# Gated attention mix on one core: the weights' last 64 rows written to both partition halves by one transfer, and one rounding step moved ahead of two evictions

## The chip, the cores and the metric

The kernel runs on one core of one Trainium2 chip. The metric is the device time of one execution in microseconds; the time before is the median of three runs.

## The reference

Two attention blocks read the same `x` (2048 positions, 448 features, 16 heads of 28), and a sigmoid gate mixes their results. Block A attends to 8 positions two apart, backwards; block B attends to all positions. Cut to what matters:

```python
g = sigmoid((x * gate_w).sum(-1, keepdims=True))
# A: q, k, v = x @ A_wqkv; position s sees s, s-2, ..., s-14 (those >= 0)
a = softmax8(q . k[s - 2w] * 28**-0.5) . v[s - 2w] @ A_wo
# B: q, k, v = x @ B_wqkv; all positions, 16 heads
b = softmax(q @ k.T * 28**-0.5) @ v @ B_wo
out = g * a + (1 - g) * b
```

## The kernel before

**Split numbers.** A float32 operand of TensorE is kept as two tiles: `hi`, rounded to the matmul's type by ScalarE, and `lo`, what is left of it, made by VectorE or GpSimd (`split`: one ScalarE activation, then one subtraction). A product takes three matmuls per block of 128 features: hi·hi, hi·lo and lo·hi.

**Features.** 448 features are three blocks of 128 rows (`kt` 0 to 2) and a tail of 64 rows (`kt` 3). The tail tile has 128 partitions: for `x` one half of the partitions holds the hi part of the 64 rows and the other half the lo part, and the weights' 64 tail rows stand in both halves. One matmul over 128 partitions then does hi·hi and lo·hi of the tail. So each weight tail is loaded twice, into partitions 0 to 63 and 64 to 127; `both` does that. `xh[nb]` and `xl[nb]` hold `x` in four blocks of 512 positions; they are loaded raw into slices of the tile `V` (`load_x`, `load_tails`) and split by `split_x(nb)`, whose kt 3 step is a 64-row activation on ScalarE and a 64-row subtraction on VectorE.

**The start.** SyncE (SP) issues, in this order: three blocks of the first weights, the tail of x block 0, the first weights' tail for columns 448 to 703 (`both`, into `wt0`), `wr1` (384 weight rows for columns 0 to 127), their tail (`both`), the tail of x block 1, then x block 1 (`load_x(1)`), block 2, the tails of blocks 2 and 3, block 3. ScalarE's own queue issues x block 0. All of SP's transfers share one queue, and each of the eight semaphores that the transfers signal is used in turn, so that SP waits, before a transfer, until the one eight places earlier has landed.

**The projections.** `tiles` lists the output tiles. Tiles 0 to 9 are projected whole (`project`); tiles 0 and 1 are interleaved product by product in the order `FIRST`, which takes kt 3 last. Tiles 0, 1 and 2 use x block 0, tiles 3 to 5 block 1, tiles 6 and later blocks 2 and 3. Tile n goes to PSUM bank `PS[n % 4]`, is evicted by `qk_tile` (one ScalarE activation, L361, one VectorE subtraction, L362) and stored to DRAM by two transfers. Both evictions of tiles 0 and 1 stand after tile 1's place in the loop, followed by `split_x(1)`, which takes kt 3 first, then 0, 1, 2. From tile 10 on the two row halves go to two banks at once (`project_halves`), and from tile 11 on S1 matmuls (L148) are put between them: a first pass of scores that finds each row's maximum, for which `KH` and `QP` are read back from DRAM. Later weights are loaded and split by `load_w` and `split_w` at tile numbers that `loads` and `splits` give; each tail goes through `both`.

**After the projections.** 256 steps each compute a piece of block B's scores (L991), their exponentials (ScalarE) and the product with V (L957), while GpSimd and VectorE work on block A from a list; the last part multiplies by the output weights. The order of the instructions on each engine is that of the code: nothing is rearranged when the kernel runs.

Of the kernel before, what the change touches and what calls it, by code (L numbers as in the profile page):

```python
# [25 lines left out]
def gated_mix_kernel(ctx: ExitStack, tc: tile.TileContext, xT, xn, gw, wA, wB, woAB, out):  # L26
    nc = tc.nc
# [170 lines left out]
    def max_turn(t):  # L198
        r = sp.tile([128, 32], F32, name="nms")
        nc.vector.transpose(r, t.bitcast(F32))  # L200
        return r
# [18 lines left out]
    with tc.tile_pool(name="xp", bufs=1) as xp, tc.tile_pool(name="wp", bufs=2) as wp:  # L220
# [3 lines left out]
        def raw3():  # L224
            return wp.tile([128, 3, 450], F32, tag="raw", name="raw", bufs=2)

        def split(hi, lo, raw, eng=nc.vector):
            nc.scalar.activation(hi, raw, AF.Copy)
            eng.tensor_tensor(out=lo, in0=raw, in1=hi.bitcast(F32), op=ALU.subtract)


        def both(dst, src, eng=nc.sync):
            for h in (0, 64):
                eng.dma_start(dst[h:h + 64], src)


        xst = V.rearrange("p j h e -> p (j h e)").rearrange("p (b k c) -> p b k c", b=NB, k=4)
# [10 lines left out]
        LOW = [slice(64, 128)] * 2 + [slice(0, 64)] * 2  # L248
        HIGH = LOW[2:] + LOW[:2]

        def split_x(nb):
            r, t = xst[:, nb, 0:3, :], xst[:, nb, 3, :]
            tail = xh[nb][:, 3, :]
            o, i = LOW[nb], HIGH[nb]
            for kt in (3, 0, 1, 2) if nb == 1 else range(4):
                if kt < 3:
                    split(xh[nb][:, kt, :], xl[nb][:, kt, :], r[:, kt, :])
                else:
                    nc.scalar.activation(tail[i], t[i], AF.Copy)
                    nc.vector.tensor_tensor(out=tail[o], in0=t[i], in1=tail[i].bitcast(F32), op=ALU.subtract)  # L260
# [3 lines left out]
        def load_w(wi, tails=(False, True)):  # L264
            src, cols = WSRC[wi]
            if wi not in wraw:
                wraw[wi] = raw3(), wp.tile([128, 450], F32, tag="wt", name="wt"), sum(c1 - c0 for c0, c1 in cols) + 2 * (wi == GATE)
            r, t, _ = wraw[wi]
            for tail in tails:
                o = 0  # L270
                for c0, c1 in cols:
                    e = o + c1 - c0
                    if tail:
                        both(t[:, o:e], src[384:448, c0:c1])
                    else:
                        nc.sync.dma_start(r[:, :, o:e], src[0:384, c0:c1].rearrange("(k p) c -> p k c", p=128))
                    o = e

                if wi == GATE:
                    if tail:  # L280
                        both(t[:, o:o + 2], gw[0:2, 384:448].rearrange("i p -> p i"))
                    else:
                        for kt in range(3):
                            nc.sync.dma_start(r[:, kt, o:o + 2],
                                              gw[0:2, 128 * kt:128 * kt + 128].rearrange("i p -> p i"))

        def split_w(wi, kts):
            if wi not in wsets:
                wsets[wi] = [wp.tile([128, 4, 450], F32R, tag=g, name=f"{g}{wi}") for g in ("wh", "wl")]
            wh, wl = wsets[wi]  # L290
            r, t, n = wraw[wi]
            for kt in kts:
                split(wh[:, kt, :n], wl[:, kt, :n], r[:, kt, :n] if kt < 3 else t[:, :n], nc.gpsimd)
# [24 lines left out]
        def project(n):  # L318
            if n == 0:
                for m, p in FIRST:  # L320
                    product(m, p, None, p == (0, 0, 0), p == (0, 1, 3))
            elif n > 1:
                for i, p in enumerate(ORDER):
                    product(n, p, None, i == 0, i == len(ORDER) - 1)
# [4 lines left out]
        def project_halves(n, s1):  # L329
            if n % 2 == 0:  # L330
                for m in (n, n + 1):
                    low = (tiles[m][2] if tiles[m][1] == "qk" else tiles[m][-1] // 4) < 2
                    for half in range(2):
                        l = [p for p in ORDER if p != (0, 1, 3) or half == (0 if low else 1)]
                        l = [(m, product, (m, p, half, i == 0, i == len(l) - 1)) for i, p in enumerate(l)]
                        if s1[m - n]:
                            l[8:8] = [(m, s1_half, (1, half))]
                            l[2:2] = [(m, s1_half, (0, half))]
                        todo[half] += l
            while any(l and l[0][0] == n for l in todo):  # L340
                for l in todo:
                    if l:
                        _, f, x = l.pop(0)
                        f(*x)
# [32 lines left out]
        def add_halves(n, dst, gate=None):  # L377
            raw = pair("raw")
            cols = D + 2 * (gate is not None)
            nc.scalar.activation(raw[:, :, 0:cols], PJ[n % 2][:, :, 0:cols], AF.Copy)  # L380
            nc.gpsimd.tensor_tensor(out=dst, in0=raw[:, 0, 0:D].rearrange("p (c e) -> p c e", e=dst.shape[-1]),  # L381
                                    in1=raw[:, 1, 0:D].rearrange("p (c e) -> p c e", e=dst.shape[-1]), op=ALU.add)
            if gate is not None:
                nc.gpsimd.tensor_tensor(out=gate, in0=raw[:, 0, D:D + 1], in1=raw[:, 1, D:D + 1], op=ALU.add)
# [38 lines left out]
        r, t = xst[:, 0, 0:3, :], xst[:, 0, 3, :]  # L423
# [35 lines left out]
        for n, t in enumerate(tiles):  # L459
            wi = t[0]  # L460
            for w in loads:
                if loads[w] == n:
                    load_w(w)
            for w in splits:
                i, k = (n - splits[w][0]) * splits[w][1], splits[w][1]
                if 0 <= i < 4:
                    split_w(w, range(i, i + k))
            if n in (3, 5):
                split_x((n + 1) // 2)
            if n < FULL:  # L470
                project(n)
            else:
                project_halves(n, [S1_START <= m < S1_START + 80 for m in (n, n + 1)])
            if t[1] == "qk":
                for m in {0: (), 1: (0, 1)}.get(n, (n,)):
                    qk_tile(m, *tiles[m][2:4])
            elif t[1] == "v":
                add_halves(n, V[:, t[2], :, 0:DH])
            else:
                a_tile(n, t[2], t[3])  # L480
            if n == 1:
                split_x(1)
            if n == 4:
                for t in QP[1]:
                    nc.scalar.activation(t, t0, AF.Copy)
            while fini and fini[0][0] <= n:
                fini.pop(0)[1]()
            if n in (2, 3):
                load_w(1, (n == 3,))
            if n == 3:  # L490
                load_qhi(0)
            if n in (3, 8):
                load_k(0, KH[0], qk_hi, slice(0, 1024) if n == 3 else slice(1024, S))
            if n == 16:
                for i in (1, 2):
                    nc.sync.dma_start(a_scr[i][:, 0:NJ, :].rearrange("c j e -> c (j e)").rearrange(
                        "c (a b) -> c a b", b=NJ), omg[0:8, None, :].to_broadcast([8, 56, NJ]))
            if n == 32:
                nc.gpsimd.memset(V[:, :, :, DH:], 1.0)
            if n == 22:  # L500
                load_k(1, KH[1], qk_hi)
            if n == 62:
                load_k(0, KL[0], qk_lo)
            if parts and parts[0][0] <= n:
                _, u, t = parts.pop(0)
                max_store(u, max_turn(t))
            if finished and n < len(tiles) - 3:
                u = finished.pop(0)
                parts.append((n + 3, u, max_parts(u)))
            if n == 64:  # L510
                gate = []
                for sgn, dst in ((-1.0, g_t), (1.0, omg)):
                    e = sp.tile([128, NJ], F32, name="ez")
                    nc.scalar.activation(e, zt, AF.Exp, scale=sgn)
                    nc.gpsimd.tensor_tensor(out=e, in0=e, in1=V[:, 0, :, DH], op=ALU.add)
                    gate.append((dst, e))
            if n in (66, 68):
                nc.vector.reciprocal(*gate.pop(0))
            if n == 70:
                nc.sync.dma_start(og_scr.rearrange("(j p) -> p j", j=NJ), omg)  # L520
            if n == 76:
                load_q(0)
# [70 lines left out]
    for nme in ("k", "v"):  # L593
        for i in range(2):
            t = a1.tile([128, HALO + NJ, 56], F32, name=f"{nme}t{i}")
# [110 lines left out]
    for c in range(8):  # L706
# [20 lines left out]
        n = 0  # L727
# [278 lines left out]
    for u in range(NU):  # L1006
        g, b = divmod(u, NB)
        for kt in range(NJ):
# [22 lines left out]
            if finished:  # L1031
                v = finished.pop(0)
                t = max_parts(v, (lambda f: at("end", st + 1, f)) if v < NU - 1 else None)
# [56 lines left out]
```

## Time and profile before

| | |
|---|---|
| median of three runs | 901.62 us (900.81 to 901.74) |
| the profiled execution | 900.95 us |
| its span in the profile | 899.2 us |
| TensorE matmul (PE) | busy 892.3 us, 99% |
| VectorE (DVE) | busy 739.0 us, 82% |
| ScalarE (ACT) | busy 643.1 us, 72% |
| GpSimd (POOL) | busy 639.7 us, 71% |
| granted TensorE clock | 1.0 |

The times in the rows are microseconds from the start of the span. In a row of the timeline stand the start, the time from the start to the end of the merged instructions, the engine, the line, the operation, out<-in, sizes and a count; a bracket at the end tells how long the engine was idle before it and what released it. PE is the matmul, PEld the loading of the stationary operand, SPq the issue of a transfer by SyncE. A DMA share is the mean busy share of the core's 16 DMA engines; it can exceed 1 because packets on an engine overlap.

### The profile page before, as it was taken

How to read it: one execution, taken by the hardware profiler on the slowest of the kernel's cores; microseconds unless marked ns; L12 is line 12 of the kernel's file. 1: busy time of each engine (PE TensorE's matmuls, PEld its weight loads, DVE VectorE, ACT ScalarE, POOL GpSimd, SP SyncE). 2: the span in 40 equal slices, each digit the busy share in tenths (PEclk: the TensorE clock that was granted, in tenths of full speed). 3: DMA queues.
4: the chain of work that ended last, by engine and by line, in shares of the span. 5: the costliest groups of instructions: out<-in, count | busy, mean ns of one | idle time of the engine just before them, and what ended most of it. 6: DMA issues, size and time to landing. Idle time of an engine off the chain costs nothing.

```text
span 899.2 us, 20532 instructions
## 1 busy us (share of the span) xinstructions
PE 892.3 (99%) x8323; PEld 525.1 (58%) x8323; DVE 739.0 (82%) x961; ACT 643.1 (72%) x765; POOL 639.7 (71%) x506
## 2 busy tenths in 40 slices
PE   9999999999999999999999999999999999999998
PEld 6888999998954444444444444444444444434997
DVE  6588999998979999999999999989999999832220
ACT  7456434343378898988988989889889898897220
POOL 1499847464459689999999999999999698501000
PEclk9999999999999999999999999999999999999999
DMA  8877403559472341226225242352220322337691
GB/s 268 284 256 197 138 12 84 143 136 95 123 239 73 100 127 46 70 57 156 70 56 145 84 115 64 88 136 65 53 64 18 94 43 56 96 81 208 183 272 52
DMA packets 115975, 104.51 MB, mean 116 GB/s; under 512 B 77177, under 2 KB 84217, under 8 KB 115097
## 3 DMA queue, kind: packets, MB, share of 16 engines
q1 hardware_dynamic: 115448, 102.42, 42.6%
q8 instruction: 65, 1.06, 0.5%
q10 hardware_dynamic: 432, 0.79, 0.3%
q14 instruction: 30, 0.24, 0.1%
HBM read 62.20 MB, written 40.96 MB: 115 GB/s over the span
## 4 chain that ended last, share of the span: by engine, by line
PE 94%; POOL 2%; DMA 1%; ACT 1%; DVE 0%; issue 0%; SPq 0%; POOLq 0%; ACTq 0%
PE T L991 29%; PE av L957 26%; PE r L316 15%; PE r L311 8%; PE T L837 8%; PE r L148 5%; PE T L148 4%; DMA rbc<-rs 1%; POOL prod L670 1%; POOL oat L675 1%; DMA vt<-a_scr 0%; POOL prod L614 0%; PE r L217 0%; ACT P L996 0%; ACT raw L380 0%
## 5 line engine op out<-in xcount | busy, mean ns | idle before, releaser
L996 ACT ACTIVATE P<-T 128x1024 f32<-128x1024 f32 x512 | 496.8, 1023 | 60.4 <-PE T L991 58.4
L154 DVE TENSOR_REDUCE MX<-T 128x1 f32<-128x512 f32 x470 | 441.8, 953 | 34.2 <-PE T L148 18.2
L957 PE MATMUL av<-P,V 128*32 128x512 f32 x2048 | 272.7, 605 | 0.0
L991 PEld LDWEIGHTS T<-QH,KH 30*128 30x128 f32 x1024 | 92.2, 181 | 231.1 <-ACT P L996 197.0
L148 PE MATMUL T<-KH,QP 28*128 28x512 f32 x704 | 219.9, 455 | 0.1
L991 PE MATMUL T<-QH,KH 30*128 30x512 f32 x1024 | 212.1, 489 | 0.6 <-DVE MX L154 0.4
L170 DVE TENSOR_REDUCE MX<-r 128x2 f32<-128x1024 f32 x160 | 192.5, 1221 | 23.9 <-PE r L148 19.9
L991 PE MATMUL T<-QH,KL 28*128 28x512 f32 x1024 | 186.7, 395 | 0.0
L991 PE MATMUL T<-QL,KH 28*128 28x512 f32 x1024 | 184.5, 392 | 0.0
L614 POOL TENSOR_TENSOR prod<-qt,kt 128x896 f32<-128x896 f32 x64 | 135.4, 2116 | 5.5 <-DMA kt<-a_scr 5.4
L380 ACT ACTIVATE raw<-r 128x896 f32<-128x896 f32 (+1 forms) x64 | 58.9, 921 | 98.0 <-PE r L316 96.4
L148 PE MATMUL r<-KH,QP 64*128 64x512 f32 x320 | 105.6, 391 | 0.0
L675 POOL TENSOR_TENSOR oat<-oat,prod 128x896 f32<-128x896 f32 x48 | 101.3, 2110 | 2.0
L148 PEld LDWEIGHTS T<-KH,QP 28*128 28x128 f32 x704 | 86.0, 181 | 27.2 <-ACT P L996 19.5
L381 POOL TENSOR_TENSOR ast<-raw 128x448 f32<-128x448 f32 x48 | 55.4, 1154 | 59.2 <-ACT raw L380 51.7
L670 POOL TENSOR_TENSOR prod<-vt,L 128x896 f32<-128x896 f32 x56 | 95.3, 1701 | 0.2
L316 PE MATMUL r<-wh,xh 64*128 64x448 f32 (+1 forms) x512 | 93.7, 363 | 0.9 <-ACT raw L380 0.9
L991 PEld LDWEIGHTS T<-QL,KH 28*128 28x128 f32 x1024 | 94.5, 184 | 0.0
L991 PEld LDWEIGHTS T<-QH,KL 28*128 28x128 f32 x1024 | 93.2, 183 | 0.3
L957 PEld LDWEIGHTS av<-P,V 128*32 128x32 f32 x2048 | 40.3, 107 | 77.7 <-issue 65.3
L316 PEld LDWEIGHTS r<-wh,xh 64*128 64x128 f32 x512 | 74.0, 185 | 4.0 <-ACT raw L380 1.3
L316 PE MATMUL r<-wh,xl 64*128 64x448 f32 (+1 forms) x384 | 73.6, 364 | 0.0
(114 smaller groups left out, 1115.6 us busy)
## 6 DMA issues: line engine op xcount, KB each, us to landing
a_scr<-ast SPq DMA_DIRECT2D x24, 448.0 KB
qk_hi<-qkh SPq DMA_DIRECT2D x24, 256.0 KB
qk_lo<-qkh SPq DMA_DIRECT2D x24, 256.0 KB
rbc<-rs SPq DMA_DIRECT2D x64, 64.0 KB
QP<-qk_hi SPq DMA_DIRECT2D x64, 56.0 KB
KL<-qk_lo SPq DMA_DIRECT2D x16, 224.0 KB
QH<-qk_hi SPq DMA_DIRECT2D x64, 56.0 KB
QL<-qk_lo SPq DMA_DIRECT2D x64, 56.0 KB
```

Source lines behind the costliest of these rows:

```text
L148: nc.tensor.matmul(bank, qhis[u][h % 2][r, 128 * qs:128 * qs + 128], KH[u // NB % 3][r, 512 * kc:512 * kc + 512], start=True, stop=True)
L154: i = nc.vector.tensor_reduce(MX[:, n % NMX:n % NMX + k], bank, axis=X, op=ALU.max)
L170: nc.vector.tensor_reduce(m, PM[k], axis=X, op=ALU.max)
L311: nc.tensor.matmul(bank, ws[c][rows, k, t[4]:t[4] + 128], x, start=first, stop=last)
L316: nc.tensor.matmul(bank[:, 0:cols], x, ws[c][rows, k, 0:cols], start=first, stop=last)
L614: nc.gpsimd.tensor_tensor(out=p, in0=qt[c], in1=kvt["k", c % 2][:, HALO - DIL * w:HALO - DIL * w + NJ, :], op=ALU.mult)
L670: nc.gpsimd.tensor_tensor(out=dst.rearrange("p j (h d) -> p j h d", d=DH), in0=kvt["v", c % 2][:, HALO - DIL * w:HALO - DIL * w + NJ, :].r ...
L675: nc.gpsimd.tensor_tensor(out=ows[c % 2][:, :, 0:56] if w == W - 1 else oat[c], in0=oat[c], in1=oat[c, w], op=ALU.add)
L837: writes(bank, nc.tensor.matmul(bank[:, :D], src, wo[c][k], start=(first and k == ks[0] and i == 0), stop=(last and k == ks[-1] and i == 2)))
L957: nc.tensor.matmul(av[32 * h:32 * h + 32, :], V[:, kt, 4 * g + h, :], tiles_[h], start=(kt == 0), stop=(kt == NJ - 1), skip_group_check=True)
L991: nc.tensor.matmul(bank[a], (KH[g % 3], KH[g % 3], KL[g % 2])[t][r, ks], (qh, ql, qh)[t][r, :], start=(t == 0), stop=(t == 2))
L996: e = nc.scalar.activation(p, one if a == "2" else mine, AF.Exp, scale=SCALE).ins
```

## The change

**One transfer in place of two.** `both(dst, src)` issued two transfers of 64 rows, one for each half of the partitions. Now it issues one with the whole tile of 128 partitions as its destination; its source is the same 64 rows taken twice, by a leading step of 0 with a count of 2. It is used nine times, so that nine transfers stand where 18 stood: two at the start, two for the two column pieces of weight set 1, one for each of sets 2 to 6. The gate's tail column is still loaded by two transfers.

**One step moved.** `split_x(1)`, called after tile 1's evictions, is cut in two: its kt 3 step now stands after the projection of tiles 0 and 1 and ahead of their evictions, its kt 0 to 2 steps where they were. Blocks 2 and 3 keep their order.

```diff
         def both(dst, src, eng=nc.sync):
-            for h in (0, 64):
-                eng.dma_start(dst[h:h + 64], src)
+            eng.dma_start(dst, src[None].to_broadcast([2, *src.shape]))
...
-        def split_x(nb):
+        def split_x(nb, kts=range(4)):
             r, t = xst[:, nb, 0:3, :], xst[:, nb, 3, :]
             tail = xh[nb][:, 3, :]
             o, i = LOW[nb], HIGH[nb]
-            for kt in (3, 0, 1, 2) if nb == 1 else range(4):
+            for kt in kts:
...
                     if tail:
-                        both(t[:, o:o + 2], gw[0:2, 384:448].rearrange("i p -> p i"))
+                        for h in (0, 64):
+                            nc.sync.dma_start(t[h:h + 64, o:o + 2], gw[0:2, 384:448].rearrange("i p -> p i"))
...
+            if n == 0:
+                split_x(1, (3,))
             if t[1] == "qk":
                 for m in {0: (), 1: (0, 1)}.get(n, (n,)):
                     qk_tile(m, *tiles[m][2:4])
...
             if n == 1:
-                split_x(1)
+                split_x(1, range(3))
```

SyncE's queue at the start, first as it stood before (`raw` and `wr` are weights, `wt` a weight tail, `V` holds raw x; the sizes are those of the destination):

```order
L409 DMA raw<-in_wB 128x256 x3
L244 DMA V<-in_xT 64x512
L234 DMA wt_191<-in_wB 64x256 x2
L413 DMA wr_192<-in_wB 128x3x128
L234 DMA wt_191<-in_wB 64x128 x2
L244 DMA V<-in_xT 64x512
L240 DMA V<-in_xT 128x3x512 x2
```

and as it stands now:

```order
L409 DMA raw<-in_wB 128x256 x3
L243 DMA V<-in_xT 64x512
L233 DMA wt_191<-in_wB 128x1x256
L413 DMA wr_192<-in_wB 128x3x128
L233 DMA wt_191<-in_wB 128x1x128
L243 DMA V<-in_xT 64x512
L239 DMA V<-in_xT 128x3x512 x2
```

The order is the same with two transfers fewer: `wr1`, the second tail and x block 1 each stand one or two places nearer to the front, and each `wt` transfer now covers 128 partitions.

ScalarE between the last split of the first weights and x block 1 (`wh` the weights' hi tile, `qkh` an evicted tile, `xh_181` x block 1, `xh_182` block 2), before:

```order
L228 ACTIVATE wh_188<-wt_191 128x256
L228 ACTIVATE wh_188<-wr_192 128x3x128
L228 ACTIVATE wh_188<-wt_191 128x128
L361 ACTIVATE qkh<-r_128 128x512
L361 ACTIVATE qkh<-r_132 128x512
L259 ACTIVATE xh_181<-V 64x512
L228 ACTIVATE xh_181<-V 128x512 x3
```

and now:

```order
L228 ACTIVATE wh_188<-wt_191 128x256
L228 ACTIVATE wh_188<-wr_192 128x3x128
L228 ACTIVATE wh_188<-wt_191 128x128
L258 ACTIVATE xh_181<-V 64x512
L361 ACTIVATE qkh<-r_128 128x512
L361 ACTIVATE qkh<-r_132 128x512
L228 ACTIVATE xh_181<-V 128x512 x3
```

The 64-row activation of x block 1 went two places up, ahead of the evictions of tiles 0 and 1; VectorE's 64-row subtraction moved in the same way ahead of its two L362 rows. TensorE's order is unchanged.

## The prediction

> **What bounds the kernel now.** I read the page first (busy shares, then the chain), and then the busy times by stretch.
>
> ```profile
> PE 892.3 (99%) x8323; PEld 525.1 (58%) x8323; DVE 739.0 (82%) x961; ACT 643.1 (72%) x765; POOL 639.7 (71%) x506
> ...
> PE 94%; POOL 2%; DMA 1%; ACT 1%; DVE 0%; issue 0%; SPq 0%; POOLq 0%; ACTq 0%
> ```
>
> ```profile
> 60.00:230.00 170.00, 169.08 (x1591) 157.44 (x1589) 153.43 (x137) 74.37 (x104) 110.90 (x118) 1.00 0.52 123
> ```
>
> TensorE is busy 99% of the span and carries 94% of the chain; from 60 to 230 us it works 169.08 of 170 us at a granted clock of 1.00. There is no idle time later in which a delay could be taken up, and none to be saved but at the start: whatever shifts TensorE's first tiles shifts the end by as much. So the change is worth what it does in the first 35 us. There I read the timeline of each engine.
>
> ```profile
> 8.76 0.40 ACT L228 ACTIVATE wh<-wt 128x256 fp32r<-128x256 f32 x1
> 9.07 0.51 ACT L228 ACTIVATE wh<-wr 128x384 fp32r<-128x384 f32 x1
> 9.48 0.30 ACT L228 ACTIVATE wh<-wt 128x128 fp32r<-128x128 f32 x1
> 10.92 1.09 ACT L361 ACTIVATE qkh<-r 128x512 fp32r<-128x512 f32 x2 [1.14 <-PE r L311]
> 11.89 0.62 ACT L259 ACTIVATE xh<-V 64x512 fp32r<-64x512 f32 x1
> 12.74 1.67 ACT L228 ACTIVATE xh<-V 128x512 fp32r<-128x512 f32 x3 [0.23 <-DMA V<-in_xT]
> ```
>
> ```profile
> 11.64 0.88 PEld L311 LDWEIGHTS r<-xh,wl 128*128 128x128 f32 x4
> 12.57 0.65 PEld L311 LDWEIGHTS r<-xl,wh 128*128 128x128 f32 x3
> 13.42 0.19 PEld L311 LDWEIGHTS r<-xh,wh 128*128 128x128 f32 x1 [0.20 <-ACT xh L228]
> 13.94 0.19 PEld L311 LDWEIGHTS r<-xh,wh 128*128 128x128 f32 x1 [0.33 <-ACT xh L228]
> 14.46 0.30 PEld L311 LDWEIGHTS r<-xh,wh 128*128 128x128 f32 x2 [0.34 <-ACT xh L228]
> ```
>
> Tile 3, the first that needs x block 1, starts at 13.42 and waits three times for ScalarE's rounding of that block: 0.20 + 0.33 + 0.34 = 0.87 us. ScalarE in turn waited 0.23 us for the block to land, at 12.74. Before that it sat idle 1.14 us ahead of the evictions, and then did the 64-row step (0.62) that the change moves.
>
> **The moved step.** It is 0.62 us on ScalarE, put into an idle 1.14.
>
> ```profile
> 10.64 0.29 DVE L229 TENSOR_TENSOR wl<-wt,wh 128x128 fp32r<-128x128 f32 x1
> 11.55 1.29 DVE L362 TENSOR_TENSOR qkh<-r,qkh 128x512 fp32r<-128x512 f32 x2 [0.62 <-ACT qkh L361]
> 12.87 0.68 DVE L260 TENSOR_TENSOR xh<-V,xh 64x512 fp32r<-64x512 f32 x1
> ```
>
> On VectorE it is 0.68 into an idle 0.62, so the evictions could be 0.06 late; their banks are next written by tile 4, three tiles on, so that costs nothing. The move frees ScalarE at 10.92 + 1.09 = 12.0 instead of 12.5; it pays only if block 1 has landed by then. What the move adds is a wait: behind the 64-row step on ScalarE now stand both evictions, block 1's rounding and all later tiles, and the step waits for the tail of block 1. So everything hangs on when transfers land.
>
> **The merged transfers.** Each saves SyncE an issue:
>
> ```profile
> 2.71 2.42 SPq L234 DMA_DIRECT2D wt<-in_wB  x2
> 5.18 0.59 SPq L413 DMA_DIRECT2D wr<-in_wB  x1
> 5.82 1.17 SPq L234 DMA_DIRECT2D wt<-in_wB  x2
> 7.03 0.59 SPq L244 DMA_DIRECT2D V<-in_xT  x1
> 7.92 0.91 SPq L240 DMA_DIRECT2D V<-in_xT  x2
> ```
>
> Two issues of 1.17 / 2 = 0.59 us go from in front of block 1 (issued at 7.92), some 1.2 us. But the bytes stay the same, and the question is how they are dealt over the 16 engines. Before, each tail was two transfers with 64 as the outermost count on both sides: 4 rows on each engine, twice. Now the destination's outermost count is 128, and the source's is 2, the two copies of the same 64 rows. If the source's count decides, two engines carry 64 rows each and 14 carry none. No row of this trace has a transfer with such unlike sides; the nearest are loads of `KH` and `KL` with an outermost count of 28, which 16 does not divide. Two stretches that hold little else give these shares of the 16 engines, the first from 287.8 to 291 us, the second from 317.6 to 321:
>
> ```profile
> q1 hardware_dynamic: 123, 0.67, 89.2%
> ...
> KH<-qk_hi SPq DMA_DIRECT2D x1, 224.0 KB
> ```
>
> ```profile
> q1 hardware_dynamic: 134, 0.75, 99.2%
> ```
>
> 28 rows dealt evenly need 14 engines, a share of 87.5% where packets do not overlap. The first agrees, the second, in which they overlap, neither proves nor refutes it. So the rows only lean to dealing by the outermost count. The Trainium skill's page "DMA: Bandwidth & Descriptors" (section "Rules for kernel authors") speaks against this change: it says that a leading zero-stride broadcast of c copies keeps a whole transfer on at most c engines; by that rule the two-engine case below is the one, and no run here shows it yet.
>
> **Two engines: the sum.** The price of a row on one engine comes from the q1 rows of three short stretches (packets, MB, share of 16 engines), of 1 KB, 512 B and 2 KB rows:
>
> ```profile
> q1 hardware_dynamic: 228, 0.21, 38.1%
> ```
>
> ```profile
> q1 hardware_dynamic: 359, 0.16, 88.4%
> ```
>
> ```profile
> q1 hardware_dynamic: 364, 0.73, 101.1%
> ```
>
> The first is 4.2 to 5.8 us: 0.381 x 16 x 1.6 us = 9.75 us over 0.21 MB / 1024 = 205 rows, 48 ns each. The second is 7.6 to 8.4: 11.3 us over 312 rows, 36 ns. The third is 9.8 to 11.8: 32.4 us over 356 rows, 91 ns. The first tail starts to move when block 0 is nearly through, which this stretch (6.2 to 7.4) shows: 12 of its 384 packets, on ScalarE's queue q10, are left.
>
> ```profile
> q1 hardware_dynamic: 324, 0.27, 101.2%
> q10 hardware_dynamic: 12, 0.01, 2.5%
> ```
>
> I take 6.4. From there each of the two engines has, in order: first tail 64 x 48 ns = 3.07 us; `wr1` 24 x 36 = 0.86; second tail 64 x 36 = 2.30; tail of block 1 4 x 91 = 0.36; block 1 24 x 91 = 2.18. Sum 8.8, so block 1's last row moves at 15.2. Before, block 1 began near 9.7, after a stretch (8.4 to 9.7) with a DMA share of only 0.68, and 9.7 + 2.18 = 11.9, while ScalarE saw it at 12.74: 0.85 us to land.
>
> ```profile
> 8.40:9.70 1.30, 1.30 (x7) 1.00 (x6) 1.27 (x3) 1.30 (x4) 0.00 (x0) 1.00 0.68 128
> ```
>
> So now it lands at 15.2 + 0.85 = 16.05, 3.3 us later than 12.74. SyncE's 1.2 us does not help, as the rows queue on the two engines. What stands ahead of it is done by then: the second tail lands at 6.4 + 6.23 + 0.85 = 13.5, its rounding takes 0.30, and tile 2, which needs it for its fourth product, ends some 8 products of 0.22 us later (the rows at 11.64 and 12.57), near 15.8; block 1's tail lands at 13.85, its step and the two evictions (0.62 + 1.09) end at 15.6. Tile 3 starts 3.3 late, and its gaps stay. Bounds: dividing the same engine times by all packets gives 43 and 31 ns, a sum of 8.0 and +2.5 us; the stretch 6.2 to 7.4 as a whole cost 19.4 us for 0.27 MB, 74 ns a KB, which for the first tail adds 1.7 and gives +5.0. I take +3.3, the middle one, since it stands on rows of the same sizes without other rows between.
>
> **Later tails.** Weight set 1's (1280 B and 256 B rows) put 56 more rows of each on the two engines: 56 x 60 + 56 x 18 to 36 ns, 4.4 to 5.4 us. They are issued at 21.04, ahead of what the first S1 matmuls read:
>
> ```profile
> 21.04 3.55 SPq L234 DMA_DIRECT2D wt<-in_wB  x4
> 24.89 3.03 SPq L99 DMA_DIRECT2D QP<-qk_hi  x4
> 28.03 1.61 SPq L99 DMA_DIRECT2D KH<-qk_hi  x4
> ```
>
> ```profile
> 26.00:28.50 2.50, 2.50 (x13) 2.03 (x12) 0.69 (x1) 1.47 (x3) 0.26 (x1) 1.00 0.33 97
> 28.50:32.00 3.50, 3.50 (x18) 2.58 (x16) 0.69 (x1) 1.49 (x4) 3.11 (x4) 1.00 0.82 259
> ```
>
> ```profile
> 34.63 0.18 PEld L148 LDWEIGHTS r<-KH,QP 64*128 64x128 f32 x1
> ```
>
> Idle DMA time of 1.7 and 0.6 us covers 2.3 of it; 2.1 is left (3.1 at the dear end), and the S1 matmul at 34.63, being 3.3 later itself, covers that. I take 0 and keep 0 to 2.1 for the range. Sets 2 to 6 (rows up to 1792 B) add at most 56 x 91 ns = 5.1 us each to two engines at a DMA share of 0.52; set 3's, for one, is read 23 us after its issue, so 0; without that cover it would be a few microseconds.
>
> ```profile
> 53.98 1.18 SPq L234 DMA_DIRECT2D wt<-in_wB  x2
> ```
>
> ```profile
> 77.36 0.57 ACT L228 ACTIVATE wh<-wt 128x448 fp32r<-128x448 f32 x1
> ```
>
> Against the profiled execution's own 900.95 us (span 899.2) the sum is 904.25; the median shown, 901.62, is 0.67 higher, and on it the forecast is 901.62 + 3.3 = 904.9.
>
> **The rivals.** *Sixteen engines.* The destination's 128 rows decide, 8 on each engine as before. Then the transfers cost what they did, block 1 is issued 1.2 us earlier and lands before 12.0, ScalarE starts it at 12.0, 0.74 earlier, and the three gaps of 0.87 us go: 900.7, no measurable change. For it: both sides name the same bytes, and the second 28-row stretch shows no idle engines. Against it: the lean of the first. It decides if the source's count does not limit the spread. The skill's same section would expect this side of the change to pay: it advises one 128-partition transfer instead of two to partition halves, since both halves use the same 16 engines anyway.
>
> *Two engines, partly hidden.* Shares over 100% show packets overlapping on an engine. If a row that no other engine competes with takes half its price, the two tails take 1.54 and 1.15 us, the sum is 6.1, block 1 lands at 13.35, 0.6 late: 902.2. Against it: the price of 48 ns hides little, as its stretch was near 100% busy.
>
> *Two engines, and S1 waits too.* The 2.1 us of set 1's tail is not covered, because SyncE waits for the transfer eight places earlier before it issues `KH`, and that is now a slow tail: 904.9 + 2.1 = 907.0. Against it: TensorE comes 3.3 us later to that place.
>
> **How the numbers follow.** Two engines as summed 0.53; with the S1 wait 0.20; partly hidden 0.08; sixteen engines 0.15; the rest 0.04. The range: from 902.1, a little under the partly hidden case, to 908.7, which is +5.0 with +2.1; it holds 0.81. Forecast alone: 904.1 (+2.5) to 906.6 (+5.0). About 0.2% (1.8 us) is what a measurement of this kernel can tell from no change. Slower by more than that: 0.53 + 0.20 and half of the rest, 0.75; within: partly hidden and most of sixteen engines, 0.21; faster: sixteen engines with an earlier issue that brings more than I see, and half of the rest, 0.04.
>
> **What would show it.** In the profile after: the first `wh<-wt` on ScalarE starts near 10.3 instead of 8.76; block 1's first rounding near 16 with a wait for `V`; tile 3's first weight load near 16.7; the DMA share between 8 and 15 us falls far below 1, few engines being busy. If instead ScalarE's 64-row step stands before 10.92 and tile 3 starts by 13.2 without its three waits, the sixteen engines were right. I am wrong on the later tails if the first L148 weight load comes more than 3.3 us after 34.63 for a wait on `KH` or `QP`.

## The result and the profile after

The changed kernel takes 905.01 us (median of six runs, 904.16 to 905.95) against 901.01 for the kernel before, run beside it on the same chip (six runs, 900.53 to 901.74). The ratio is 1.0043, with an interval of 1.0031 to 1.0056: slower by 3.9 us (2.8 to 5.0). The forecast was 904.9, 3.3 us slower. The profiled execution took 905.43 us, with a span of 903.7.

The page of after, busy shares and the chain by engine:

```profile
PE 894.4 (99%) x8323; PEld 529.0 (59%) x8323; DVE 739.2 (82%) x961; ACT 643.6 (71%) x765; POOL 639.9 (71%) x506
...
PE 93%; POOL 4%; DMA 1%; ACT 1%; SPq 1%; issue 0%; DVE 0%; POOLq 0%; DVEq 0%; ACTq 0%
```

The work is the same, and TensorE still carries the chain; SyncE's issues (SPq) rose from 0% to 1% of it. The time was lost at the start, as ScalarE's timeline of after shows:

```profile
11.30 0.42 ACT L228 ACTIVATE wh<-wt 128x256 fp32r<-128x256 f32 x1 [2.12 <-DMA wt<-in_wB]
11.91 0.53 ACT L228 ACTIVATE wh<-wr 128x384 fp32r<-128x384 f32 x1 [0.19 <-DMA wr<-in_wB]
13.84 0.31 ACT L228 ACTIVATE wh<-wt 128x128 fp32r<-128x128 f32 x1 [1.40 <-DMA wt<-in_wB]
14.07 0.63 ACT L258 ACTIVATE xh<-V 64x512 fp32r<-64x512 f32 x1
14.61 1.06 ACT L361 ACTIVATE qkh<-r 128x512 fp32r<-128x512 f32 x2
16.16 1.67 ACT L228 ACTIVATE xh<-V 128x512 fp32r<-128x512 f32 x3 [0.49 <-DMA V<-in_xT]
```

Both tails of the start are now waited for (2.12 and 1.40 us, where ScalarE waited for neither before). The moved 64-row step (14.07) stands ahead of the two evictions (14.61), and x block 1 is rounded at 16.16 instead of 12.74, 3.42 later. TensorE's weight loads of after, for tile 3 and for the first S1 matmul:

```profile
16.84 0.19 PEld L311 LDWEIGHTS r<-xh,wh 128*128 128x128 f32 x1 [0.95 <-ACT xh L228]
17.36 0.19 PEld L311 LDWEIGHTS r<-xh,wh 128*128 128x128 f32 x1 [0.34 <-ACT xh L228]
17.88 0.30 PEld L311 LDWEIGHTS r<-xh,wh 128*128 128x128 f32 x2 [0.34 <-ACT xh L228]
...
38.05 0.18 PEld L148 LDWEIGHTS r<-KH,QP 64*128 64x128 f32 x1
```

Tile 3 starts at 16.84 instead of 13.42, +3.42, and keeps its three waits, the first of them 0.95 instead of 0.20. At the first S1 matmul the lag is still 38.05 - 34.63 = 3.42.

Most of it was lost before tile 3, at the tails themselves. TensorE's matmuls of after, up to tile 2's last three products, then those three in before:

```profile
11.77 0.74 PE L311 MATMUL r<-xh,wh 128*128 128x512 f32 x2 [1.07 <-ACT wh L228]
...
14.20 0.50 PE L311 MATMUL r<-xh,wh 128*128 128x512 f32 x1 [0.54 <-ACT wh L228]
...
15.47 0.85 PE L311 MATMUL r<-xl,wh 128*128 128x512 f32 x3
```

```profile
12.80 0.86 PE L311 MATMUL r<-xl,wh 128*128 128x512 f32 x3
```

TensorE waits for the rounding of the two tails (1.07 and 0.54 us), and tile 2's last products come 15.47 - 12.80 = 2.67 late; the wait for x block 1 brings that to 3.42.

The busy times by stretch (time, then PE, PEld, DVE, ACT, POOL, granted clock, DMA share, GB/s), first of before, then of after:

```profile
8.00:11.00 3.00, 3.00 (x14) 1.95 (x13) 2.81 (x6) 1.86 (x7) 0.00 (x0) 1.00 0.81 231
```

```profile
8.00:11.00 3.00, 2.71 (x12) 1.87 (x10) 1.71 (x3) 1.19 (x3) 0.00 (x0) 1.00 0.39 92
11.00:15.00 4.00, 2.69 (x10) 1.84 (x11) 1.54 (x4) 2.11 (x5) 0.00 (x0) 1.00 0.97 325
8.00:15.00 7.00, 5.40 (x22) 3.71 (x21) 3.25 (x7) 3.29 (x8) 0.00 (x0) 1.00 0.72 225
```

From 8 to 11 us the share fell from 0.81 to 0.39; the 16 engines had too little to do while ScalarE waited. Within that time, the transfers of after from 8.5 to 9.8 us (busy share by slice in tenths, then packets, MB, share of 16 engines):

```profile
DMA  0110010011001100100110011001001100110010
...
q1 hardware_dynamic: 59, 0.06, 13.4%
```

13.4% of 16 engines are 2.1 engines. They moved 59 rows of 1 KB: 0.134 x 16 x 1.3 us / 59 = 47 ns of one engine for each, the price that the prediction took (48). So two engines were at work on the first tail and 14 were idle. The sizes of the trace's packets say the same: of the 384 rows of 512 B of `wr1`, 336 had started by 7.7 us, 14 times the 24 that 384 rows make for each of 16 engines, and no row of that size started again until 9.8; the other 48, two engines' share, stood behind the first tail.

SyncE's queue in after shows why the others were given nothing more to do:

```profile
2.72 0.66 SPq L233 DMA_DIRECT2D wt<-in_wB  x1
4.73 0.40 SPq L413 DMA_DIRECT2D wr<-in_wB  x1
5.17 0.55 SPq L233 DMA_DIRECT2D wt<-in_wB  x1
5.77 3.49 SPq L243 DMA_DIRECT2D V<-in_xT  x1
9.30 1.32 SPq L239 DMA_DIRECT2D V<-in_xT  x2
```

The issue of the tail of x block 1, 0.59 us before, took 3.49. x block 1 was thus issued at 9.30, later than before (7.92), although two issues fewer stood in front of it.

### The profile page after: what moved, and what is told of

It reads as the page before. It is cut to its first block, busy times and chain, and to the rows that moved or that the text cites. A ratio compares the mean times of both kernels' runs of the same rounds, so it can differ in the third digit from the quotient of the medians.

```text
span 903.7 us, 20517 instructions
## 1 busy us (share of the span) xinstructions
PE 894.4 (99%) x8323; PEld 529.0 (59%) x8323; DVE 739.2 (82%) x961; ACT 643.6 (71%) x765; POOL 639.9 (71%) x506
## 4 chain that ended last, share of the span: by engine, by line
PE 93%; POOL 4%; DMA 1%; ACT 1%; SPq 1%; issue 0%; DVE 0%; POOLq 0%; DVEq 0%; ACTq 0%
PE T L993 29%; PE av L959 26%; PE r L316 15%; PE T L839 8%; PE r L311 7%; PE r L148 4%; PE T L148 3%; DMA V<-in_xT 1%; POOL prod L616 1%; POOL prod L672 1%; POOL oat L677 1%; POOL prod L621 0%; SPq L243 0%; ACT P L998 0%; ACT raw L380 0%
## 5 line engine op out<-in xcount | busy, mean ns | idle before, releaser
L148 PE MATMUL T<-KH,QP 28*128 28x512 f32 x704 | 219.7, 454 | 0.1
L148 PEld LDWEIGHTS T<-KH,QP 28*128 28x128 f32 x704 | 86.0, 181 | 27.1 <-ACT P L998 19.2
L148 PE MATMUL r<-KH,QP 64*128 64x512 f32 x320 | 86.4, 392 | 0.0
L316 PE MATMUL r<-wh,xh 64*128 64x448 f32 (+1 forms) x512 | 82.3, 363 | 1.2 <-ACT raw L380 1.2
L621 POOL TENSOR_TENSOR prod<-prod 128x448 f32<-128x448 f32 x64 | 65.7, 1026 | 5.0
L316 PE MATMUL r<-wh,xl 64*128 64x448 f32 (+1 forms) x384 | 69.2, 364 | 0.0
```

Source lines behind the costliest of these rows:

```text
L148: nc.tensor.matmul(bank, qhis[u][h % 2][r, 128 * qs:128 * qs + 128], KH[u // NB % 3][r, 512 * kc:512 * kc + 512], start=True, stop=True)
L316: nc.tensor.matmul(bank[:, 0:cols], x, ws[c][rows, k, 0:cols], start=first, stop=last)
L621: nc.gpsimd.tensor_tensor(out=lo, in0=lo, in1=hi, op=ALU.add)
```

## The experiments

The theory: a transfer whose source has the 64 rows twice by a step of 0 runs on two engines, and that makes the start late; the moved step is worth nothing either way. Rivals: the moved step costs (its new wait holds both evictions); or a transfer over 128 partitions with the work on all 16 engines would cost as much. A second question is whether the later tails cost anything. Each ratio below is to the kernel before, run beside that kernel on the same chip.

**The move alone.** `both` issues two transfers again, the step stays moved.

```diff
-            eng.dma_start(dst, src[None].to_broadcast([2, *src.shape]))
+            for h in (0, 64):
+                eng.dma_start(dst[h:h + 64], src)
```

> The step is moved, but every weight tail is still loaded by two transfers of 64 rows. If the two-engine dealing of the merged transfer is the cause (theory D), nothing of the 4 us is left: x block 1 is issued and lands as before (near 12.7 us), so tile 3 starts near 13.4 and the time is that of the kernel before, 0 to -0.2 us. If the moved step holds up the evictions and what stands behind them (rival M), this kernel alone is slower, by up to 3 or 4 us.

Measured: 900.33 us against 900.33 (ratio 0.9999, 0.999 to 1.0008). The timeline of ScalarE, then of the weight loads, in this run:

```profile
11.34 0.63 ACT L259 ACTIVATE xh<-V 64x512 fp32r<-64x512 f32 x1 [1.64 <-DMA V<-in_xT]
11.88 1.05 ACT L362 ACTIVATE qkh<-r 128x512 fp32r<-128x512 f32 x2
13.07 1.67 ACT L228 ACTIVATE xh<-V 128x512 fp32r<-128x512 f32 x3
```

```profile
13.75 0.19 PEld L312 LDWEIGHTS r<-xh,wh 128*128 128x128 f32 x1 [0.59 <-ACT xh L228]
```

The step does add a wait (1.64 us for the tail of block 1), the evictions go behind it, and block 1's rounding starts at 13.07 instead of 12.74. But tile 3 comes only 0.33 later than before, and the median shows none of it.

**The merge alone.** `split_x(1)` in one piece after the evictions, as before.

```diff
-            if n == 0:
-                split_x(1, (3,))
...
-                split_x(1, range(3))
+                split_x(1, (3, 0, 1, 2))
```

> The tails are loaded by one transfer with the rows taken twice, and the 64-row step stands behind the evictions as before. Theory D: +3.5 to +4.5 us, all of the change's loss, with the first tail seen by ScalarE near 11.3 us and x block 1 near 16. Rival M: near 0.

Measured: 904.52 us, ratio 1.0048 (1.0036 to 1.0061), that is +4.3 us, the whole loss. ScalarE at x block 1, and SyncE:

```profile
15.67 1.67 ACT L228 ACTIVATE xh<-V 128x512 fp32r<-128x512 f32 x3 [0.52 <-DMA V<-in_xT]
```

```profile
5.74 3.08 SPq L243 DMA_DIRECT2D V<-in_xT  x1
8.87 1.30 SPq L239 DMA_DIRECT2D V<-in_xT  x2
```

The held issue is there again (3.08 us). The loss belongs to the merge; the move is out.

**One transfer, the rows twice in DRAM.** Two more inputs hold each weight's last 64 rows twice, 128 rows one behind the other; the transfer's source then has 128 as its outermost count, as the destination has. The step stays moved.

```diff
-            eng.dma_start(dst, src[None].to_broadcast([2, *src.shape]))
+            eng.dma_start(dst, src)
...
-                        both(t[:, o:e], src[384:448, c0:c1])
+                        both(t[:, o:e], (tA if src is wA else tB)[:, c0:c1])
```

> One transfer per tail as in the change, but its source holds the 64 rows twice in DRAM (two more inputs, the last 64 rows of each weight matrix laid out twice), so that both sides have 128 as the outermost count. The step is moved as in the change. Theory D: dealt over 16 engines, 8 rows each; x block 1 is issued near 6.5 and lands near 11.8, tile 3 starts near 12.7 to 13.2, and the time is 0.5 to 0.9 us below the kernel before. Rival S (one transfer of 128 rows into a tail tile is slow of itself, or SyncE's fewer issues do harm): as slow as the change, +4.

Measured: 900.61 us, ratio 1.0001 (0.9992 to 1.0009). SyncE, then the weight loads:

```profile
5.82 0.47 SPq L243 DMA_DIRECT2D V<-in_xT  x1
6.33 1.12 SPq L239 DMA_DIRECT2D V<-in_xT  x2
```

```profile
13.82 0.88 PEld L311 LDWEIGHTS r<-xh,wh 128*128 128x128 f32 x4
```

One transfer in place of two costs nothing that these runs resolve, so the loss isn't in the merging but in the source's form. Block 1 is issued 1.6 us earlier (6.33), and tile 3's three waits are gone. The gain of 0.5 to 0.9 us that I expected from that is not seen; the interval (-0.7 to +0.8) would just hold the small end of it. In this profiled run tile 3 starts at 13.82, 0.40 later than before, in spite of it, because TensorE's first matmuls were slower, here in this run and then in before:

```profile
5.46 1.17 PE L311 MATMUL r<-xh,wh 128*128 128x512 f32 x2
```

```profile
5.40 0.62 PE L311 MATMUL r<-xh,wh 128*128 128x512 f32 x2
```

**How many engines.** The source's leading count was varied with the bytes of each destination row kept: 64 (the step of 0 inside), 8 and 4.

```diff
-            eng.dma_start(dst, src[None].to_broadcast([2, *src.shape]))
+            eng.dma_start(dst, src[:, None].to_broadcast([64, 2, src.shape[1]]))              # 64
+            eng.dma_start(dst, src[None, 0:16].to_broadcast([8, 16, src.shape[1]]))           # 8
+            eng.dma_start(dst, src[None, 0:32].to_broadcast([4, 32, src.shape[1]]))           # 4
```

> One transfer per tail whose source also takes every row twice by a step of 0, but with the two steps in the other order: 64 outermost, 2 inside. Row i of the tail then stands in partitions 2i and 2i + 1, so the output is not the reference's; bytes, rows and the number of transfers are those of the change. Theory D: 16 engines, time as with the rows laid out twice in DRAM, 0.5 to 0.9 us below the kernel before. Rival B (reading rows twice by a step of 0 is what is slow): as slow as the change, +4 us.

> As with 4, but the first 16 rows taken eight times (the output is not the reference's): eight engines carry 16 rows each, 1.35 us in place of 5.4, x block 1 lands near 12.3, and the time is that of the kernel before or some tenths below, -0.5 to +0.3 us. If only counts that 16 divides spread, +4 us.

> One transfer per tail of as many rows and bytes as in the change, with 4 as the source's outermost count: the first 32 of the 64 rows, taken four times (so the tails' content and the output are not the reference's). If the source's outermost count sets the number of engines, four engines carry 32 rows each: 32 x 48 + 32 x 36 ns = 2.7 us in place of 5.4, so that x block 1 lands near 13.4 instead of 16.1, and the time is +0.6 us (0 to +1.2). If anything but a count of 64 falls back to two engines or one, +4 or more.

Measured: 64: 900.49 us, ratio 1.0000 (0.9992 to 1.0009). 8: 899.97, 0.9997 (0.9988 to 1.0006). 4: 902.95, 1.0030 (1.0019 to 1.0042), +2.7 us. ScalarE at x block 1 with 8, and with 4; then SyncE with 4:

```profile
12.94 1.67 ACT L228 ACTIVATE xh<-V 128x512 fp32r<-128x512 f32 x3 [0.19 <-DMA V<-in_xT]
```

```profile
14.78 1.67 ACT L228 ACTIVATE xh<-V 128x512 fp32r<-128x512 f32 x3 [0.88 <-DMA V<-in_xT]
```

```profile
5.71 0.51 SPq L243 DMA_DIRECT2D V<-in_xT  x1
6.26 1.11 SPq L239 DMA_DIRECT2D V<-in_xT  x2
```

A step of 0 as such does no harm: inside, under a count of 64, it is free, though the 0.5 to 0.9 us that I expected to gain are not in the median here either. The leading count sets the loss: 2 gives block 1 at 16.16, 4 at 14.78, 8 at 12.94, 64 at 12.05, where before had 12.74. With 4 I was wrong: I took +0.6 (0 to 1.2) and it was +2.7. Halving the rows on an engine took the lag from 3.42 only to 2.04: the first tail was taken at 10.10, where 6.4 + 1.54 + 0.85 gives 8.8. Whether the later tails have a share in the 2.7 is not shown; TensorE's lag in the profiled run grows by no more than 0.05 from tile 3 to 180 us. The run with 4 also parts two causes: there SyncE isn't held (0.51), block 1 is issued at 6.26, 1.66 earlier than before, and still it lands 2 us late. So the rows queued on the few engines make the start late; the held issue is not needed for it. What the hold adds with a count of 2 was not tried by itself. The Trainium skill's page "DMA: Bandwidth & Descriptors" (section "Rules for kernel authors") says that a leading broadcast of c copies, with c under 16, keeps the transfer on at most c engines; the 2.1 engines of after agree with it, and so do the losses with 2, 4 and 8 copies (+3.9 us, +2.7 us and none).

**The start alone, the later tails alone.** `both` goes by whether later weights have been begun (`wraw`); the step stays moved.

```diff
         def both(dst, src, eng=nc.sync):
+            if len(wraw):     # later tails as two transfers; in the other kernel: if not wraw
+                for h in (0, 64):
+                    eng.dma_start(dst[h:h + 64], src)
+                return
             eng.dma_start(dst, src[None].to_broadcast([2, *src.shape]))
```

> The two tails at the start are merged as in the change, the seven later ones are loaded by two transfers as before; the step is moved. If the loss is made at the start (the sum on record: +3.3), +3.4 us remain. If the later tails make the other part of the 4 us (in the profile of the change TensorE lost another 0.4 us near 88 us, after ScalarE had waited for stores to land), this kernel is 0.4 to 0.8 us faster than the change; if that part was chance, it is as slow, +3.9.

> The mirror image: the tails at the start by two transfers, the seven later ones merged as in the change; the step is moved. By the sum on record the later tails cost 0 (0 to 2.1). If TensorE's later 0.4 us come from them, +0.4 to +0.8 us here; x block 1 lands as in the kernel before.

Measured: the start alone 902.93 us, ratio 1.0032 (1.0019 to 1.0044), +2.9 (1.7 to 4.0). The later tails alone 901.94, 1.0021 (1.0012 to 1.0030), +1.9 (1.1 to 2.7), more than the 0.4 to 0.8 that I had expected of them. The two add up to 4.8, which the intervals let stand beside the 3.9 of the whole.

Where do the later tails cost? In after, SyncE behind set 3's tail, with the one row of before that stands for the same issue:

```profile
57.39 0.53 SPq L233 DMA_DIRECT2D wt<-in_wB  x1
...
59.70 4.49 SPq L498 DMA_DIRECT2D a_scr<-omg  x2
64.29 3.00 SPq L99 DMA_DIRECT2D qk_hi<-qkh  x1
```

```profile
56.31 1.53 SPq L496 DMA_DIRECT2D a_scr<-omg  x2
```

The same hold as at the start: 4.49 us for two issues that took 1.53. Behind them stand the stores of the evicted tiles, and ScalarE's timeline of after waits for those stores, as it never did before:

```profile
68.26 1.03 ACT L366 ACTIVATE raw<-r 128x1024 f32<-128x1024 f32 x1 [1.85 <-DMA qk_lo<-qkh]
...
102.12 0.92 ACT L380 ACTIVATE raw<-r 128x896 f32<-128x896 f32 x1 [2.74 <-DMA qk_lo<-qkh]
```

So I guessed set 3 (the tail at 57.39) and tried it alone, the other later sets without it, and set 3 alone on ScalarE's queue; the two tails of the start and the order of `split_x(1)` are those of the kernel before in all three.

```diff
+            if one:
+                eng.dma_start(dst, src[None].to_broadcast([2, *src.shape]))
+                return
...
-                        both(t[:, o:e], src[384:448, c0:c1])
+                        both(t[:, o:e], src[384:448, c0:c1], one=wi == 3)       # or wi != 3
```

> Before, with one transfer in place of two for weight set 3's tail alone (the one issued at 53.98 us); the start and the other sets as before. Theory A (set 3's slow tail holds SyncE, the stores behind it land late, ScalarE waits for buffers of L366, and TensorE loses some 0.4 us near 90 us and some near 215): SyncE's issue of a_scr or of a store behind the tail takes 2.5 us or more in place of 0.7 to 1.5, ScalarE L366 waits for the store of qk_lo by 1.5 to 3 us in all between 60 and 120 us, and the time is +0.4 to +1.0 us. Rival B (the later loss is spread over all sets): no such wait, +0 to +0.3 us.

> Before, with one transfer in place of two for the tails of weight sets 1, 2, 4, 5 and 6; the start and set 3 as before. Theory A (the later loss comes from set 3): no wait of ScalarE L366 for a store between 60 and 120 us, and 0 to +0.5 us. Rival B (spread over all sets): +1.0 to +1.9 us, what the kernel with all the later tails merged showed.

> Set 3's tail alone as one transfer, issued by ScalarE on its own queue instead of by SyncE; all else as before. If the tail's harm comes from standing ahead of the stores in SyncE's queue, SyncE's issues behind it are short again (under 2 us), ScalarE waits under 1 us for a store between 60 and 120 us, and the time is -0.2 to +0.4 us. If two busy engines alone do the harm, through the stores' own rows on them, L366 waits for the stores as it does with the tail on SyncE (1.5 to 3 us) and the time is as in the run with set 3 alone, +0.4 to +1.0.

Measured: set 3 alone 900.78 us, ratio 1.0010 (1.0001 to 1.0019), +0.9. The others without it 901.24, 1.0013 (1.0005 to 1.0022), +1.2. Set 3 on ScalarE's queue 900.39, 1.0005 (0.9996 to 1.0014). SyncE and ScalarE with set 3 alone:

```profile
56.31 4.36 SPq L499 DMA_DIRECT2D a_scr<-omg  x2
60.77 2.94 SPq L99 DMA_DIRECT2D qk_hi<-qkh  x1
```

```profile
67.10 1.03 ACT L369 ACTIVATE raw<-r 128x1024 f32<-128x1024 f32 x1 [0.64 <-DMA qk_lo<-qkh]
```

and with set 3 on ScalarE's queue:

```profile
56.13 2.33 SPq L499 DMA_DIRECT2D a_scr<-omg  x2
```

```profile
66.70 1.03 ACT L369 ACTIVATE raw<-r 128x1024 f32<-128x1024 f32 x1 [1.07 <-PE r L314]
```

Set 3's tail holds SyncE by itself (4.36 us), and off SyncE's queue both the hold and the wait for a store are smaller or gone. But the wait was only 0.64 us instead of the 1.5 to 3 expected, and the other sets, without any such wait in the profile, cost +1.2, inside what the rival gave. My theory that set 3 is the whole cause falls: by the medians it is +0.9 (0.1 to 1.7), and +1.2 (0.5 to 2.0) belongs to the other sets. The run on ScalarE's queue settles little: its interval reaches from -0.4 to +1.3 us, and its tail was issued 4.7 us earlier (49.30), which helps by itself.

## Why the prediction was right, and where not

**Two engines instead of sixteen: right**, seen directly (13.4% of 16 engines, 47 ns a row), and the sixteen-engine case, tried with the rows twice in DRAM, gave what that rival said: no measurable change.

**The sum at the start: right in total, with two errors that cancel.** The first tail was forecast for 10.3 and was taken at 11.30, 1.0 late; the second for 13.5, taken at 13.84; x block 1 for 16.05, taken at 16.16; tile 3 for 16.7, begun at 16.84. The trace's packets show both errors. The first tail began near the 6.4 that I took, but was slower at first: fewer than 20 of its 128 rows had started by 7.5, and from there they went near the price of the sum, up to 10.4. What follows it was cheaper: 13.84 - 11.30 = 2.5 us for `wr1` and the second tail, where I had 0.86 + 2.30 = 3.2, since the last 48 rows of `wr1` began at 9.8, before the first tail had ended. Tile 2, too, was done later than I had it (15.47 + 0.85 = 16.3 against 15.8): by this trace the tails alone cost 2.67 of the 3.42, and the wait for block 1 only the rest. The start alone measured +2.9 (1.7 to 4.0) beside the forecast +3.3.

That 904.9 lands so near 905.01 is in part luck: it was counted from 901.62, and the kernel before, with more runs, has 901.01; a loss that was 0.6 larger than forecast (3.9 against 3.3) made up for a base that was 0.6 too high.

**SyncE's saved issues: wrong in sign.** I had block 1 issued 1.2 us earlier, without use. It was issued 1.38 later (9.30), held by its neighbour. The run with a count of 4 shows that block 1 is late without it too.

**The DMA share from 8 to 15 us: half right.** "Far below 1" holds from 8 to 11 (0.39); over the whole stretch it is 0.72.

**The later tails: mis-sized.** The term was 0, with 0 to 2.1 for the range, and it rested on set 1 and the S1 matmuls. That part held: L148 starts 3.42 later, no more than tile 3, so the rival with a wait on `KH` and `QP` is out. But by themselves the later tails cost +1.9 (1.1 to 2.7). The step that failed was to ask only when a tail itself is read ("set 3's, for one, is read 23 us after its issue, so 0"), and not what stands behind it in SyncE's queue: stores, for whose buffers ScalarE waits. For set 3 the profiled run of after shows how this reaches TensorE. The rows are one addition on GpSimd (POOL) in before, the same one in after, and a weight load of TensorE in after:

```profile
65.49 1.31 POOL L368 TENSOR_TENSOR raw<-raw 128x512 f32<-128x512 f32 x1
```

```profile
69.36 1.29 POOL L368 TENSOR_TENSOR raw<-raw 128x512 f32<-128x512 f32 x1 [0.40 <-ACT raw L366]
```

```profile
90.14 0.30 PEld L316 LDWEIGHTS r<-wh,xh 64*128 64x128 f32 x4 [0.39 <-ACT raw L366]
```

ScalarE's evictions are late by the wait for the store (1.85 us at 68.26), so GpSimd waits 0.40 for them and starts 69.36 - 65.49 = 3.87 late, where the lag had been 3.42. From there to 90 us GpSimd is never idle (busy 20.60 of 20.60 us from 69.4 to 90.0) and does not make it up; ScalarE waits for GpSimd, and TensorE for ScalarE's eviction, 0.39 at 90.14. Behind that TensorE's lag is 3.87. The same wait of TensorE, 0.82 and 0.45 us, stands in the runs of the merge alone and of the later tails alone; no profiled run in which set 3's tail is on 16 engines, or on four or eight, has it. With set 3 alone, where ScalarE waited 0.64 in place of 1.85, TensorE's lag grows there by only 0.1. The wait of 2.74 at 102.12 is not seen in TensorE, whose lag stays at 3.87 up to 180 us.

By 218 us the lag of after is 4.47, at the same matmul in before and in after:

```profile
213.54 0.67 PE L316 MATMUL r<-wh,xh 64*128 64x448 f32 x4 [0.92 <-ACT raw L380]
```

```profile
218.01 0.68 PE L316 MATMUL r<-wh,xh 64*128 64x448 f32 x4 [1.22 <-ACT raw L380]
```

That makes all of the 905.43 - 900.95 = 4.48 between the two profiled executions. But this last 0.6 is not shown to come from the tails: the wait at this place also differs between runs whose later tails are not merged (0.92 in before, 0.30 with the move alone, none with the start alone). How the +1.2 of the sets without set 3 comes about stays open.

## What to carry to other kernels

Fewer transfers is not the same as less transfer time: look at the outermost count of both sides, since a source that repeats a block twice by a leading step of 0 ran on two engines here, and the engines' rows queue up in front of all that follows. If one transfer is wanted, put a large count outermost, for example by storing the rows twice. And cost a slow transfer not by its own reader but by everything behind it on the same queue, stores and the buffers that they free among it; a short wait stays in the time when it reaches an engine that has no idle time behind it, as GpSimd here.

## What the runs showed of the hardware that was not expected

An issue on SyncE is not of fixed length: behind two transfers on two engines it took 3.49 and 3.08 us instead of 0.59, and with four or eight engines 0.51. That the queues of the two engines were full is the likely reason, but no run shows it.

One transfer over 128 partitions instead of two over 64 brought no gain that these runs resolve (ratio 1.0001, 0.9992 to 1.0009), although it saves an issue each time; the Trainium skill advises it on the page "DMA: Bandwidth & Descriptors" (section "Rules for kernel authors"), and here it brought the issue of x block 1 forward by 1.6 us and left the measured time as it was.

TensorE's first two matmuls of tiles 0 and 1 (5.4 us) took 0.93 to 1.17 us instead of 0.62 in ten of the thirteen profiled runs, at a granted clock of 1.00 in the profile's rows. That is the pace of the nine matmuls ahead of them (4.11 us in before, 0.46 each), and in after it lasts to about 7 us. It moves the start by some 0.5 us from run to run. All seven runs with one transfer per tail at the start have it, and three of the six with two, so whether the merge has a part in it is not shown, and its cause is open.
